# fp16 high and low parts, scaled by powers of two found on the chip, in place of 32-bit ones

## The chip, the core and the metric

The kernel runs on one core of a Trainium2 chip. The metric is the device time of one execution in microseconds (us). TensorE (PE) multiplies matrices, VectorE (DVE) and ScalarE (ACT) work elementwise, GpSimd (POOL) does small integer work and issues the gathers, SyncE (SP) issues nearly all other transfers. Every engine takes its instructions strictly in the order of the program, and waits for the others by semaphores.

## What is computed

```python
def _A_ref(x, wq, wk, wv, wo):            # attention: 32 heads of 16, one key and one value head
    q, k, v = heads(x @ wq), x @ wk, x @ wv
    p = _softmax(einsum("bhqd,bkd->bhqk", q, k) * (Dh ** -0.5), axis=-1)
    return merge(einsum("bhqk,bkd->bhqd", p, v)) @ wo

def _B_ref(x, w_q, k1, k2, u, v):         # 4096 experts, picked by two tables of 64 keys, 32 heads
    q = jnp.einsum("nd,dhc->nhc", xf, w_q)
    s1 = jnp.einsum("nhd,ed->nhe", q[..., :dk], k1)
    s2 = jnp.einsum("nhd,ed->nhe", q[..., dk:], k2)
    # the best two of s1 and of s2, and of their four sums the best two: top_s, top_e
    g = _softmax(top_s, axis=-1)
    act = _gelu(jnp.einsum("nd,nhkd->nhk", xf, u[top_e]))
    return jnp.einsum("nhk,nhk,nhkd->nd", g, act, v[top_e])

xn = _layernorm(x, axis=-1)               # x is 2048 x 512
return x + _A_ref(xn, A_wq, A_wk, A_wv, A_wo) + _B_ref(xn, B_w_q, B_k1, B_k2, B_u, B_v)
```

## The kernel before

**Stages.** The 2048 rows of x are 16 tiles of 128, in four groups of four. A prologue normalises each group, transposes it on PE (`transpose_group`) and forms keys, values and queries. Then 256 steps of attention follow (the loop over `d`, `att_steps`): in each, four pairs of score products (`scores`, L412) go to ACT, which takes their exponential (L419, 1024 columns each), and 16 products with the values (`pv`, L429) follow one step later. All other work is laid between these, by a list that the program writes out when it is built: PE gets a "fill" behind the second pair of scores of each step (`run_scores`), and ACT gets what stands in the list `ON_ACT` between the two pairs of exponentials (`mid`).

**Experts.** For the chunk `c` (four heads of eight chunks) `wp_make` multiplies the key tables into the query weights: four products (L583) of raw tiles of 512 KB (`wqt`, loaded by `wp_load` four tiles ahead into five buffers that are used in turn), four ACT copies (L584), and four transposes (L590), each of which ACT and DVE split into a high and a low part (L592, L593). These parts (`wk`) are stored to HBM (`dw`, L599) and read again for the later groups of rows (`wp_read`, L605). `item` forms the scores of one tile and one chunk in twelve products of 512 columns (L631); DVE takes the best of each head (L644, L646). For the first two groups of rows, the picked rows of u and v are gathered by index (L1091), multiplied and summed on DVE (L1103, L1138). For the other two, `dense` computes all 4096 experts: one-hot products build a table of gates (L892 to L895, L925), then for each of 32 blocks of 128 experts rows of u and v are loaded and split (`half_split`, L797, L798), multiplied with the transposed x (L833), gated, split (`high`, `low`: L1030, L1034), and multiplied with v (L971); DVE adds the results to the totals (L974).

**High and low parts.** A factor `a` of these products is held as a high part `h` and a low part `a - h`, and three of the four cross products are summed, so that twelve products stand for four. Before, the parts are 4-byte numbers (type fp32r): the rounding in the copy makes `h`, and a DVE subtraction makes the low part. Transposed x, the scores' weights, the query and key weights, u, v and the gated activations are held so.

**Transfers.** Everything that SP issues goes in order through one hardware queue (q1): among it the raw tiles, the stored and reread parts, the rows of u and v for `dense`, and for each pair of attention units a chain `dsum`, `rc`, `dinv`, `rsb` (L447 to L473) that turns the softmax's sums around through HBM for DVE's division (L478). The gathers go through a queue of their own (q0).

The names that the steps below use: `scale_factors` and `weight_squares` (prologue, one factor for the keys and queries), `wp_make` (chunks), `half_split`, `sums` and `first` (dense part), `gate`s of `batch`.

## Time and profile before

| | us |
|---|---|
| three runs, median (lowest to highest) | 1819.83 (1819.26 to 1823.11) |
| the profiled execution, its own time | 1823.24 |
| its span, first to last instruction | 1821.5 |
| of that busy: PE / DVE / ACT / POOL | 1743.2 / 1625.8 / 1290.0 / 698.9 |
| longest chain of work, share by engine | PE 48%, DVE 32%, DMA 6%, issue 4%, ACT 3% |
| moved by DMA | 478.31 MB |

The profile is that of one execution. A busy PE overlaps the modelled ends of its products, so 96% is not its peak. The trace tells the stages apart by the lines that run in them: prologue to 120 us, gathers with `wp_make` to about 320, gathers with stored parts to 560, one-hot tables to 700, the first dense part to 1010, scores of the second and fourth group to 1330, and then the one-hot and dense part of the last group.

### The profile page before, as it was taken

Reading aid. Unit: us, or ns where it says so; the run is one execution under the profiler, and the core shown is the slowest. Engines: PE = TensorE matmul, PEld = TensorE weight load, DVE = VectorE, ACT = ScalarE, POOL = GpSimd, SP = SyncE. Lnnn points to the kernel's source line nnn. Section 1 sums busy time; section 2 is a strip of 40 time slices with the busy share of each in tenths; the row PEclk is TensorE's granted clock in tenths of the full one; section 3 lists DMA queues with packets and bytes.
Section 4 is the critical chain, followed back from the end, with each engine's and each line's share of the span. In section 5 each row is a group of like instructions: output and inputs, shape, how many; then the busy total and the mean of one; then the engine's idle time right before and its main releaser. Section 6 shows DMA issues by size and latency. Waiting matters only on the chain.

```text
span 1821.5 us, 34944 instructions
## 1 busy us (share of the span) xinstructions
PE 1743.2 (96%) x10997; PEld 880.0 (48%) x10997; DVE 1625.8 (89%) x6385; ACT 1290.0 (71%) x1750; POOL 698.9 (38%) x922
## 2 busy tenths in 40 slices
PE   7999999999998889999999999999988899999998
PEld 4644444555554334555555444555543344555553
DVE  7749989999899977999999798999989778999994
ACT  5367766656568987888787565556689877888874
POOL 1124544435442122444444353345521124444440
PEclk9999999999999999999999999999999999999999
DMA  8489897996764777988899987877636768898883
GB/s 287 175 303 376 303 339 248 347 336 237 242 201 132 238 243 223 284 276 290 283 313 325 321 311 240 291 249 249 229 98 232 251 189 292 286 308 286 286 283 105
DMA packets 243705, 478.31 MB, mean 263 GB/s; under 512 B 93748, under 2 KB 117316, under 8 KB 243516
## 3 DMA queue, kind: packets, MB, share of 16 engines
q0 software_dynamic: 73728, 268.47, 43.6%
q1 hardware_dynamic: 169372, 206.93, 34.2%
q8 instruction: 87, 1.43, 0.3%
q14 instruction: 102, 0.84, 0.1%
q10 hardware_dynamic: 416, 0.66, 0.1%
HBM read 419.94 MB, written 51.15 MB: 259 GB/s over the span
## 4 chain that ended last, share of the span: by engine, by line
PE 48%; DVE 32%; DMA 6%; issue 4%; ACT 3%; POOL 1%; SPq 1%; DVEq 0%; ACTq 0%; POOLq 0%
PE psc L631 16%; PE pv L429 13%; PE sc L412 8%; DVE xa L1138 7%; DVE g L1103 6%; PE pact L833 3%; DVE oh L892 3%; PE pout L971 3%; DVE i L646 2%; DVE da L974 2%; PE pwo L527 2%; ACT pt L419 2%; DVE wk L798 1%; PE pw L583 1%; DMA rsb<-dinv 1%
## 5 line engine op out<-in xcount | busy, mean ns | idle before, releaser
L419 ACT ACTIVATE pt<-sc 128x1024 f32<-128x1024 f32 x1024 | 995.9, 1030 | 379.5 <-PE sc L412 317.8
L1091 POOL DMA_INDIRECT g<-in_uv_dram,idx x512 | 561.0, 1096 | 894.7 <-DVE xa L1138 410.7
L429 PE MATMUL pv<-pt,vaug 128*32 128x512 f32 x4096 | 494.2, 600 | 0.0
L631 PE MATMUL psc<-wk,xt 128*128 128x512 f32 x1536 | 392.8, 403 | 6.9 <-DVE i L646 1.9
L1138 DVE SCALAR_TENSOR_TENSOR xa<-g,w,xa 128x512 f32<-128x512 f32 x512 | 373.5, 748 | 0.1
L412 PE MATMUL sc<-qa,kaug 64*128 64x512 f16 x2048 | 319.6, 382 | 27.6 <-ACT pt L419 22.5
L1103 DVE CUSTOM_DVE_ANT_0 g<-g,xa 128x512 f32<-128x512 f32 x512 | 336.3, 686 | 6.0 <-DMA g<-in_uv_dram,idx 5.9
L631 PEld LDWEIGHTS psc<-wk,xt 128*128 128x128 f32 x1536 | 277.2, 188 | 112.1 <-issue 42.2
L412 PEld LDWEIGHTS <-kaug 64*128 64x128 f16 x2048 | 82.4, 94 | 346.2 <-issue 341.3
L429 PEld LDWEIGHTS pv<-pt,vaug 128*32 128x32 f32 x4096 | 107.0, 109 | 254.9 <-issue 254.9
L646 DVE FIND_INDEX8 i<-m,psc 128x8 uint32<-128x64 f32 x1024 | 207.2, 227 | 0.0
L971 PE MATMUL pout<-wk,wd 128*128 128x512 f32 x768 | 195.2, 401 | 2.7 <-DVE gy L1014 1.5
L833 PE MATMUL pact<-xt,wk 128*128 128x512 f32 x768 | 196.8, 401 | 0.6 <-DVE da L974 0.6
L971 PEld LDWEIGHTS pout<-wk,wd 128*128 128x128 f32 x768 | 140.6, 188 | 49.5 <-issue 5.6
L833 PEld LDWEIGHTS pact<-xt,wk 128*128 128x128 f32 x768 | 139.3, 188 | 49.6 <-issue 18.7
L644 DVE MAX8 m<-psc 128x8 f32<-128x64 f32 x1024 | 146.5, 218 | 10.5 <-PE psc L631 10.1
L798 DVE TENSOR_TENSOR wk<-rw,wk 128x512 fp32r<-128x512 f32 x128 | 85.6, 688 | 8.1 <-ACT wk L797 8.1
L974 DVE TENSOR_TENSOR da<-da,pout 128x512 f32<-128x512 f32 x128 | 82.8, 685 | 6.2 <-PE pout L971 6.2
L892 DVE TENSOR_TENSOR oh<-oh 128x2048 f16<-128x2048 f16 x64 | 78.1, 1220 | 3.3 <-issue 1.9
L646 DVE MATCH_VALUE_LOAD i<-m,psc 128x8 f32 x1024 | 77.7, 76 | 0.0
L797 ACT CAST wk<-rw 128x512 fp32r<-128x512 f32 x128 | 74.4, 636 | 0.0
L690 POOL CAST fi<-i 128x64 f32<-128x64 uint32 x32 | 9.0, 281 | 136.7 <-DVE i L646 131.8
(179 smaller groups left out, 1341.9 us busy)
## 6 DMA issues: line engine op xcount, KB each, us to landing
wk<-dw SPq DMA_DIRECT2D x96, 512.0 KB
wqt<-in_wqT_dram SPq DMA_DIRECT2D x32, 512.0 KB
dw<-wk SPq DMA_DIRECT2D x32, 512.0 KB
rw<-in_ub_dram SPq DMA_DIRECT2D x64, 256.0 KB
rw<-in_vb_dram SPq DMA_DIRECT2D x64, 256.0 KB
gy<-dg SPq DMA_DIRECT2D x64, 256.0 KB
dg<-gst SPq DMA_DIRECT2D x14, 928.0 KB
g<-in_uv_dram,idx POOLq DMA_INDIRECT x512
```

What stands on the lines that cost most here:

```text
L412: nc.tensor.matmul(p[:, b, :], kaug[o:o + 64, kc * P:(kc + 1) * P], QA[u][o:o + 64, i, :], start=True, stop=True)
L419: nc.scalar.activation(PT[u, kc, i], p, AF.Exp, scale=SCALE)
L429: nc.tensor.matmul(PV[u][32 * j:32 * j + 32, :], vaug[:, kc, :], pt[:, b, :], start=kc == 0, stop=kc == 15)
L631: nc.tensor.matmul(p, XT[k][:, a, j * P:(j + 1) * P], WC[n_][k][:, bb, :], start=n == 0, stop=n == 11)
L644: nc.vector.max(m8[:, jb, s, :], p[:, s * E:(s + 1) * E])
L646: nc.vector.max_index(i8[:, jb, s, :], m8[:, jb, s, :], p[:, s * E:(s + 1) * E])
L833: nc.tensor.matmul(p, us[:, a, k * P:(k + 1) * P], XT[k][:, c, :], start=n == 0, stop=n == 11)
L892: nc.vector.tensor_tensor(out=oa, in0=num(P), in1=bc(0, tb, P), op=OP.is_equal)
L971: nc.tensor.matmul(p, wd[0][:, a, j * P:(j + 1) * P], vs[:, c, :], start=n == 0, stop=n == 5)
L1091: nc.gpsimd.indirect_dma_start(out=gt, out_offset=None, in_=uv, in_offset=bass.IndirectOffsetOnAxis(ap=IDX[ph, c, ti][:, s:s + 1], axis=0))
L1103: nc.vector.tensor_tensor_reduce(u, u, XN[TPH * ph + ti], scale=1.0, scalar=0.0, op0=OP.mult, op1=OP.add, accum_out=a[:, i:i + 1])
L1138: nc.vector.scalar_tensor_tensor(acc, v, w[:, i:i + 1], acc, op0=OP.mult, op1=OP.add)
```

## The change

All these parts become 2-byte fp16. Since fp16 holds a narrow range of sizes, each factor is first multiplied by a power of two that the kernel finds from norms of the data. Rows of x are scaled by 1024 in the normalisation. For the query and key weights, sums of squares give the factors (`scale_factors`, now ahead of the first split, with the products inside the first `transpose_group`). For each chunk of the raw tiles ACT sums squares (`wp_square`, 32 times, 1024 columns) and a small product on PE and three DVE operations make the factor (`wp_factors`). For u and v, all 4096 rows of `uv` (16 MB) are read once in 16 transfers of 1 MB in steps 8 to 38 of the attention, ACT sums their squares (64 times, 512 columns), and `norm_factors` makes the factors at step 43. Copies that made high parts become activations with a scale from a column of `cols`; subtractions that made low parts, and the additions of L974, become `scalar_tensor_tensor` with such a column. The inverse factors enter where values leave the products: in the exponential's, the square's and tanh's scale and in constants. The stored parts `dw` and `dxt` take half the bytes. Products with fp16 are issued as two instructions, LDWEIGHTS and MATMUL.

```diff
+XUP = 1024.0
+GDOWN = 2.0 ** -20
-    d_xt = [[dram.tile([P, 2, 512], F32, name=f"dxt{g}_{k}") for k in range(KC)] for g in range(1, NGRP)]
+    d_xt = [[dram.tile([P, 2, 512], F16, name=f"dxt{g}_{k}") for k in range(KC)] for g in range(1, NGRP)]
-    d_w = [dram.tile([P, KC, 2, 512], F32, name=f"dw{c}") for c in range(NC)]
+    d_w = [dram.tile([P, KC, 2, 512], F16, name=f"dw{c}") for c in range(NC)]
...
-                xt = big.tile([P, 2, 512], F32R, name="xt", bufs=4)
+                xt = big.tile([P, 2, 512], F16, name="xt", bufs=4)
...
     def scale_factors():
+        for k in range(KC):
+            nc.tensor.matmul(q, ones, sk[:, k, :], start=k == 0, stop=k == KC - 1)
+        nc.tensor.matmul(r, ones, st, start=True, stop=True)
         for k in range(KC):
             nc.tensor.matmul(p, ones, sq[:, k, :], start=k == 0, stop=k == KC - 1)
...
+        factors(x[:, :3], col(S_WQ, 3), col(I_Q, 3), ())
...
+    def wp_square():
+        n = squared[0]
+        squared[0] += 1
+        nc.scalar.activation(junk, WC["raw", n // 4, n % 4], AF.Square, accum_out=squares[:, n % 4:n % 4 + 1])
+
+    def wp_step(c, n=None):
+        if factored[0] < squared[0] // 4:
+            wp_factors()
+        if n is not None:
+            while squared[0] <= n:
+                wp_square()
+        n = squared[0]
+        if n < 4 * (c + 2) and n // 4 == factored[0] and ("raw", n // 4, n % 4) in WC:
+            wp_square()
+
+    def wp_factors():
+        c = factored[0]
+        factored[0] += 1
+        p = xtile("pn")[:, :1]
+        for h in range(4):
+            nc.tensor.matmul(p, ones_f, squares[:, h:h + 1], start=h == 0, stop=h == 3)
+        x = small.tile([P, 1], F32, name="xw")
+        nc.scalar.activation(x, p, AF.Copy, scale=col(K2))
+        factors(x.bitcast(I32), col(S_W + c), col(I_W + c), ())
...
     def wp_make(c):
...
                 if ("raw", n // 4, n % 4) not in WC:
                     wp_load(n // 4, n % 4)
+            wp_step(c, 4 * c + h)
             w = WC.pop(("raw", c, h))
...
-            nc.scalar.copy(wk[:, 0, :], p)
-            low = lambda p=p, wk=wk: nc.vector.tensor_tensor(out=wk[:, 1, :], in0=p, in1=wk[:, 0, :], op=OP.subtract)
+            nc.scalar.activation(wk[:, 0, :], p, AF.Copy, scale=col(S_W + c))
+            low = lambda p=p, wk=wk: nc.vector.scalar_tensor_tensor(wk[:, 1, :], p, col(S_W + c), wk[:, 0, :],
+                                                                    op0=OP.mult, op1=OP.subtract)
...
         def half_split(b, i):
             rw, w = raws[b], wk_tile()
-            nc.scalar.copy(w[:, 0, :], rw[:, i, :])
-            behind(lambda: nc.vector.tensor_tensor(out=w[:, 1, :], in0=rw[:, i, :], in1=w[:, 0, :], op=OP.subtract))
+            f = col(S_U + i)
+            nc.scalar.activation(w[:, 0, :], rw[:, i, :], AF.Copy, scale=f)
+            behind(lambda: nc.vector.scalar_tensor_tensor(w[:, 1, :], rw[:, i, :], f, w[:, 0, :],
+                                                          op0=OP.mult, op1=OP.subtract))
...
-                nc.vector.tensor_add(acc, acc, p)
+                stt(acc, p, col(C_OUT), acc, op0=OP.mult, op1=OP.add)
...
+    def norm_rows(j):
+        t = late[0].tile([P, 2, 2 * D], F32, name="un", tag="wd", bufs=2)
+        nc.sync.dma_start(t, uv[2 * j * P:2 * (j + 1) * P, :].rearrange("(r p) d -> p r d", p=P))
+        return t
+
+    def norm_sums(j, t):
+        for r in range(2):
+            for i in range(2):
+                v = t[:, r, i * D:(i + 1) * D]
+                nc.scalar.activation(v, v, AF.Square, accum_out=norms[:, i, 2 * j + r:2 * j + r + 1])
...
+    def norm_steps(d):
+        if d >= 8 and d % 2 == 0 and d // 2 - 4 < NB // 2:
+            NU[d // 2 - 4] = norm_rows(d // 2 - 4)
+        j = d // 2 - 5
+        if d % 2 == 1 and j in NU:
+            t = NU.pop(j)
+            on_act(lambda: norm_sums(j, t))
+        if d == 2 * (NB // 2 + 5) + 1:
+            norm_factors()
```

Two places of the order of instructions that the prediction speaks of. The first is ACT about 40 us into the attention, in the fourth chunk of `wp_make`: `pt` are the exponentials, `wt` the copies of the chunk's products. Before:

```order
L419 ACTIVATE pt_2049<-sc_2046 128x1024
L419 ACTIVATE pt_2054<-sc_2051 128x1024
L584 COPY wt_2065<-pw_2069 128x512
L419 ACTIVATE pt_2098<-sc_2095 128x1024
L419 ACTIVATE pt_2103<-sc_2100 128x1024
L1119 ACTIVATE gth_2113<-gy_2033 128x4
L683 ACTIVATE ex_1986<-mx_1983 128x16
L419 ACTIVATE pt_2142<-sc_2139 128x1024
L419 ACTIVATE pt_2147<-sc_2144 128x1024
L584 COPY wt_2065<-pw_2151 128x512
L584 COPY wt_2066<-pw_2164 128x512
```

Now, the same stretch, with `junk,squares` the sums of squares of raw tiles:

```order
L450 ACTIVATE pt_2124<-sc_2121 128x1024
L608 ACTIVATE junk_162,squares_163<-wqt_2137 128x1024
L645 COPY wt_2135<-pw_2140 128x512
L450 ACTIVATE pt_2169<-sc_2166 128x1024
L450 ACTIVATE pt_2174<-sc_2171 128x1024
L1184 ACTIVATE gth_2184<-gy_2103 128x4
L746 ACTIVATE ex_2056<-mx_2053,cols_159 128x16
L450 ACTIVATE pt_2213<-sc_2210 128x1024
L450 ACTIVATE pt_2218<-sc_2215 128x1024
L608 ACTIVATE junk_162,squares_163<-wqt_2220 128x1024
L645 COPY wt_2135<-pw_2223 128x512
L608 ACTIVATE junk_162,squares_163<-wqt_2234 128x1024
```

Each copy now has a square of a raw tile ahead of it, and that tile is the one four places on in the loads, which is the tile whose transfer the program issues in the same place.

The second place is SP at the same time: `wqt` are the raw tiles, `dw` the stored parts, `un` the rows of u and v that are read for their norms. Before:

```order
L599 DMA dw2_90<-wk_2007 128x1024
L567 DMA wqt_2067<-in_wqT_dram 128x2x512
L567 DMA wqt_2149<-in_wqT_dram 128x2x512
L567 DMA wqt_2162<-in_wqT_dram 128x2x512
L567 DMA wqt_2236<-in_wqT_dram 128x2x512
L447 DMA dsum_102<-e_2189 4x512
```

Now:

```order
L662 DMA dw2_90<-wk_2077 128x1024
L598 DMA wqt_2137<-in_wqT_dram 128x2x512
L598 DMA wqt_2220<-in_wqT_dram 128x2x512
L598 DMA wqt_2234<-in_wqT_dram 128x2x512
L1298 DMA un_2244<-in_uv_dram 128x2x1024
L598 DMA wqt_2311<-in_wqT_dram 128x2x512
```

The raw tiles stand where they stood, behind the last part stored, and a transfer of 1 MB has come between the third and the fourth of them; such a transfer now stands in every second step.

More of the change, by code (lines that the diff above doesn't have):

```diff
@@ L197, in transpose_group @@
             XK.setdefault(g, []).append(xt)
+            between(k)
             if not first:
@@ L203, in tile_kernel, with factors @@
     FIRST = ((0, 0), (1, 0), (0, 1))
-    sqk = const.tile([P, 2], F32, name="sqk")
+    cols = const.tile([P, 40], F32, name="cols")
+    col = lambda i, n=1: cols[:, i:i + n]
+    S_WQ, S_WKV, X_2, I_Q, I_KV, X_5, K2, G_QK, C_Q, C_K, S_Q, S_K = range(12)
+    S_U, S_V, C_SQ, C_TANH, C_OUT = range(12, 17)
+    S_W, I_W = 24, 32
+    def factors(x, scale, inverse, more):
+        nc.vector.tensor_scalar(x, x, 24, 23, op0=OP.logical_shift_right, op1=OP.logical_shift_left)
+        nc.vector.tensor_scalar(scale.bitcast(I32), x, -1.0, 205.0 * ONE, op0=OP.mult, op1=OP.add)
+        for out, power in ((inverse, -10),) + more:
+            nc.vector.tensor_scalar(out.bitcast(I32), x, (49.0 + power) * ONE, None, op0=OP.add)
     qmax = const.tile([P, NGRP], F32, name="qmax")
@@ L293, in weight_squares @@
             nc.scalar.activation(sq[:, 2 * i:2 * i + 2, :], wraws[i], AF.Square)
[L294 to L300 removed]
+            if i == 0:
+                sk = PK["ksq"] = start.tile([P, KC, 32], BF16, name="wksq")
+                nc.scalar.activation(sk, wkv_f, AF.Square)
+                st = PK["tsq"] = start.tile([P, 2 * E], BF16, name="ktsq")
+                nc.scalar.activation(st, kTs.rearrange("p s e -> p (s e)"), AF.Square)
@@ new lines, in scale_factors, with balance @@
+        x = most.bitcast(I32)
+        factors(x[:, :3], col(S_WQ, 3), col(I_Q, 3), ())
+        PK["exponents"] = x
+    def balance():
+        x = PK.pop("exponents")
+        d = start.tile([P, 1], I32, name="xd")
+        nc.vector.tensor_tensor(out=d, in0=x[:, 2:3], in1=x[:, 0:1], op=OP.subtract)
+        nc.vector.tensor_scalar(d, d, 0.5, 127.0 * ONE, op0=OP.mult, op1=OP.add)
+        sq, sk = col(S_Q).bitcast(I32), col(S_K).bitcast(I32)
+        nc.vector.tensor_single_scalar(sq, d, EXPONENT, op=OP.bitwise_and)
+        nc.vector.tensor_scalar(sk, sq, -1.0, 254.0 * ONE, op0=OP.mult, op1=OP.add)
+        nc.vector.tensor_mul(cols[:, C_Q:C_Q + 2], cols[:, S_Q:S_Q + 2], cols[:, I_Q:I_Q + 2])
+        nc.vector.tensor_mul(col(G_QK), col(I_Q), col(I_KV))
@@ L1027, in high @@
                 if not both:
-                    both.append(late[0].tile([P, 4, 512], F32R, name="wd", tag="wd", bufs=2))
+                    both.append(late[0].tile([P, 4, 512], F16, name="wd", tag="wd", bufs=2))
                 wd.append(both[0][:, 2 * half:2 * half + 2, :])
```

128 lines of the change are left out of this document (70 added, 58 removed).

## The prediction

> **What bounds the kernel now.** I read first the page's head, then the busy time of each engine in slices of 50 us, then the chain of work that ended last, stage by stage.
>
> ```profile
> span 1821.5 us, 34944 instructions
> PE 1743.2 (96%) x10997; PEld 880.0 (48%) x10997; DVE 1625.8 (89%) x6385; ACT 1290.0 (71%) x1750; POOL 698.9 (38%) x922
> ```
>
> PE is busy for nearly all of the span, which alone says little. The slices (busy us of 50 with instruction counts, then the granted clock, the DMA engines' share and GB/s) show three kinds of stage:
>
> ```profile
> 150.00:200.00 50.00, 49.04 (x289) 21.21 (x289) 46.41 (x238) 34.78 (x48) 25.25 (x36) 1.00 0.96 352
> 400.00:450.00 50.00, 50.00 (x301) 26.22 (x294) 46.48 (x308) 30.10 (x38) 23.31 (x50) 1.00 0.74 255
> 1600.00:1650.00 50.00, 49.81 (x288) 27.07 (x289) 50.00 (x121) 41.42 (x61) 22.47 (x20) 1.00 0.90 288
> ```
>
> At 150 and 400 us PE is full and DVE has 3.5 us of 50 left. At 150 us the transfers are full too (0.96), ACT has 15 us left. At 1600 us, in the second dense part, DVE is full and PE only seems so. The clock is 1.00 in all three. The chain says the same; of each stage, the shares of its own length:
>
> ```profile
> by line: PE psc L631 31.9%; PE pv L429 23.0%; PE sc L412 13.0%; PE pw L583 10.6%; DVE xa L1138 3.7%; issue 3.3%; PE pwt L590 2.9%; DVE i L646 2.9%; DVE g L1103 2.7%; DVE m L644 1.9%; DVE wk L593 1.7%; ACT pt L419 0.9%; ACT wk L592 0.8%; DVE
> by line: PE psc L631 37.2%; PE pv L429 17.7%; PE sc L412 10.6%; DVE i L646 8.0%; DMA rsb<-dinv 5.8%; DVE m L644 5.2%; DVE xa L1138 3.9%; DVE g L1103 3.5%; issue 1.6%; POOL e L730 0.7%; ACT pt L419 0.5%; POOL fi L690 0.4%; POOL ii L731 0.4%;
> by line: DVE xa L1138 12.2%; PE pact L833 10.7%; PE pout L971 9.5%; PE pv L429 9.3%; DVE g L1103 9.2%; issue 5.7%; PE sc L412 5.7%; DMA dinv<-rc 5.5%; DVE da L974 4.5%; ACT pt L419 3.4%; DMA rsb<-dinv 3.2%; DVE gy L1017 3.2%; DVE wk L798 3.
> by line: PE psc L631 43.9%; PE pv L429 23.7%; PE sc L412 14.0%; PE pwo L527 4.5%; DMA rsb<-dinv 3.1%; DVE i L646 3.0%; DVE xa L1138 2.5%; DVE g L1103 2.3%; DVE m L644 2.0%; DVE on L478 0.2%; PE pact L833 0.2%; DVE gy L1113 0.1%; DVE gg L711
> by line: DVE xa L1138 14.8%; DVE g L1103 12.9%; issue 8.8%; PE pact L833 7.7%; PE pv L429 7.4%; PE pout L971 6.5%; DVE da L974 5.3%; DMA g<-in_uv_dram,idx 5.3%; PE sc L412 4.5%; DVE wk L798 4.5%; DVE gy L1017 3.4%; DVE gy L1014 3.2%; POOL g
> ```
>
> In order: gathers with `wp_make`; gathers with stored parts; first dense part; second scoring stage; second dense part. In the first, second and fourth PE sets the pace, and ACT is on the chain for 2% at most; in the fifth DVE does; in the third both.
>
> **The change part by part.** Sums are against the profiled execution (1823.24 us, span 1821.5); it lies 0.2% above the median of 1819.83, and the sum is carried over to the median.
>
> *Faster products.* How much sooner one product follows another:
>
> ```profile
> L631 PE MATMUL psc<-wk,xt 128*128 128x512 f32 x1536 | 392.8, 403 | 6.9 <-DVE i L646 1.9 <-DMA wk<-dw 1.3 <-DVE m L644 1.1
> L833 PE MATMUL pact<-xt,wk 128*128 128x512 f32 x768 | 196.8, 401 | 0.6 <-DVE da L974 0.6
> L971 PE MATMUL pout<-wk,wd 128*128 128x512 f32 x768 | 195.2, 401 | 2.7 <-DVE gy L1014 1.5 <-DVE wd L1034 0.8 <-DVE da L974 0.3
> L302 PE MATMUL pws<-wsq,ones 128*128 128x512 bf16 x4 | 1.0, 382 | 0.0
> L925 PE MATMUL pg<-oh 128*128 128x64 f16 x960 | 37.9, 193 | 12.0 <-DVE oh L895 11.9
> 402.03 4.41 PE L631 MATMUL psc<-wk,xt 128*128 128x512 f32 x18
> 17.05 1.04 PE L302 MATMUL pws<-wsq,ones 128*128 128x512 bf16 x4
> ```
>
> Eighteen fp32r products took 4.41 us, the last of them 0.403, so one starts every (4.41 - 0.403) / 17 = 0.236 us. The four bf16 products of the prologue, also 128 by 512, each with its own weight load: (1.04 - 0.382) / 3 = 0.219. The trace has no fp16 product of full size; this is the nearest row. The gain is between 0 and 0.017 us a product, and I take 0.014. That fp16 needs two instructions costs nothing: the 960 fp16 pairs of L925 came every 37.9 / 960 = 0.039 us. Some 3300 products change (1536 + 768 + 768 and those of the prologue), 46 us in all, but only what lies on the chain counts. With 0.24 us each, the chain holds 82 us of L631 in 340 to 560 (37.2% of 220), about 340 products, 4.8 us; 140 us in 1010 to 1330, 585 products, 8.2 us; 63 us of L833 and L971 in 700 to 1010, 260 products, 3.7 us; 70 us in 120 to 340, 4.1 us. DVE is close behind in all of these (3.5 us of 50), so I take half in the second stage (-2.4), two thirds in the fourth, where DVE has more room (-5.4), half in the first dense part (-1.8), and nothing but 0.5 in the last.
>
> *DVE operations with a column as factor.* 128 of L798, 128 of L974 and 32 of L593 turn from a plain add or subtract to an operation with a scalar read from a column, which L1138 already is:
>
> ```profile
> L1138 DVE SCALAR_TENSOR_TENSOR xa<-g,w,xa 128x512 f32<-128x512 f32 x512 | 373.5, 748 | 0.1
> L974 DVE TENSOR_TENSOR da<-da,pout 128x512 f32<-128x512 f32 x128 | 82.8, 685 | 6.2 <-PE pout L971 6.2
> L798 DVE TENSOR_TENSOR wk<-rw,wk 128x512 fp32r<-128x512 f32 x128 | 85.6, 688 | 8.1 <-ACT wk L797 8.1
> 411.23 2.07 DVE L1138 SCALAR_TENSOR_TENSOR xa<-g,w,xa 128x512 f32<-128x512 f32 x3
> 1613.35 1.88 DVE L974 TENSOR_TENSOR da<-da,pout 128x512 f32<-128x512 f32 x3
> ```
>
> One of L1138 starts every (2.07 - 0.748) / 2 = 0.661 us, one of L974 every (1.88 - 0.685) / 2 = 0.598. So each costs 0.063 more, and each dense part, with 64 and 64 of them, 8.1 us of DVE. In the second nearly all of it is on the chain: +7. In the first, where DVE has half of the chain: +4. ACT's copies become scaled ones too, but ACT is not bound there.
>
> *Half the bytes.* Loads and stores of split parts shrink to half. Two waits of DVE for a small transfer stood behind such loads in SP's queue:
>
> ```profile
> 486.45 0.67 SPq L473 DMA_DIRECT2D rsb<-dinv  x1
> 499.21 0.69 DVE L478 TENSOR_TENSOR on<-ot,rsb 128x512 f32<-128x512 f32 x1 [4.48 <-DMA rsb<-dinv]
> 1008.95 0.67 SPq L473 DMA_DIRECT2D rsb<-dinv  x1
> 1019.07 0.69 DVE L478 TENSOR_TENSOR on<-ot,rsb 128x512 f32<-128x512 f32 x1 [9.92 <-DMA rsb<-dinv]
> ```
>
> `rsb` was 12.8 us on its way at 486 us and 10.1 at 1009, and DVE stood idle for 4.48 and 9.92 us. With half the bytes ahead of it most of that goes; next late are DVE's own queue and PE. Between 0 and 14.4; I take two thirds: -3 in the second stage, -6.6 in the fourth.
>
> *Prologue.* The factor now precedes the split: two squares, reductions and five small operations stand ahead of the high parts.
>
> ```profile
> 9.36 1.14 ACT L1347 CAST wqs<-g 128x512 fp32r<-128x512 f32 x2 [1.12 <-DMA g<-in_wq_dram]
> 14.77 2.01 ACT L293 ACTIVATE wsq<-g 128x1024 bf16<-128x1024 f32 x2
> 18.12 0.69 DVE L306 TENSOR_REDUCE most<-pws 128x1 f32<-128x512 f32 x1 [1.32 <-PE pws L302]
> ```
>
> Before, ACT split the weights at 9.36 us, as soon as they had come. Now 2.0 us of squares, 0.7 of the long reduction and about 1 of small ones come first, while PE transposes anyway; the first products come some 2.5 us later. The 60 products of each of four groups give 3.4 back, and the new small ones cost 1: zero.
>
> *Squares of the raw tiles and of u and v: the step that decides.* 22 of the 32 squares of 1024 columns (1.05 us each by L293) and the norms' groups of four (4 x 0.57 by the casts, 2.3 us) fall into the attention, on an engine whose exponentials PE awaits at once. ACT's gaps, and the loads:
>
> ```profile
> 155.18 1.94 ACT L419 ACTIVATE pt<-sc 128x1024 f32<-128x1024 f32 x2 [0.92 <-PE sc L412]
> 157.39 0.59 ACT L584 COPY wt<-pw 128x512 f32<-128x512 f32 x1 [0.26 <-PE pw L583]
> 159.35 1.94 ACT L419 ACTIVATE pt<-sc 128x1024 f32<-128x1024 f32 x2 [1.37 <-PE sc L412]
> 161.86 1.95 ACT L419 ACTIVATE pt<-sc 128x1024 f32<-128x1024 f32 x2 [0.38 <-PE sc L412]
> 163.69 0.59 ACT L584 COPY wt<-pw 128x512 f32<-128x512 f32 x1
> 165.51 0.59 ACT L584 COPY wt<-pw 128x512 f32<-128x512 f32 x1 [1.23 <-PE pw L583]
> 166.82 1.94 ACT L419 ACTIVATE pt<-sc 128x1024 f32<-128x1024 f32 x2 [0.72 <-PE psc L631]
> 157.09 8.78 SPq L567 DMA_DIRECT2D wqt<-in_wqT_dram  x4
> q1 hardware_dynamic: 3406, 8.05, 41.6%
> ```
>
> From 157.12, the end of one pair of exponentials, to 159.35 ACT had 1.64 us besides the copy; from 163.81 to 166.82 it had 1.95 besides two. Now a square stands ahead of each copy, so one or two in such a gap. Work alone, from 120 to 290 us: 22 squares and 8 groups of norms, 41 us, against about 16 gaps of 1.8 us and 8 of 0.4, 32: 9 us over. Behind a late square stand the next exponentials. PE waits 0.4 us later than they do (the bracket at 161.86): its next score products need the two PSUM buffers that the exponentials empty, and in all 14 such places that takes 5 off.
>
> The rest is a wait for data. Each square reads a raw tile that SP's queue is asked for in the same place of the program: before, nobody read it for another chunk, some 30 us. The queue moved 8.05 MB in 50 us, so 512 KB take 3.3 us alone, and the 256 KB of `rsb` above took up to 12.8 behind others. I take 5: its own time and half of one transfer ahead. Of the 16 such squares (chunks five to eight), three open a chunk, where the load is only issued with the copies (157.09 against 157.12), and wait 4; five stand second in a gap, on a tile whose buffer is only freed by the product just before, and wait 5 less a square, a copy and the queue's lead, 2.6; the other eight have most of a step (7 us) and wait 0.5, since the 1 MB of u and v is now ahead of some. That is 12 + 13 + 4 = 29 us. With 9 - 5 and 4.1 us less of PE, 29; not every delay is passed on whole, and I take nine tenths: **+26**. Without any wait it would be 0, with a lag of 8 us 60 instead of 29, so +54.
>
> *Factors of u and v.* At step 43 PE's small product waits for a DVE reduction that stands behind the search of a whole tile, its maxima and then their indices, which take longer:
>
> ```profile
> 403.74 1.15 DVE L644 MAX8 m<-psc 128x8 f32<-128x64 f32 x8 [1.42 <-PE psc L631]
> ```
>
> That is +3, once.
>
> Sum: 0 + 26 + (-2.4 - 3 + 3) + (4 - 1.8) + (-5.4 - 6.6) + (7 - 0.5) = **+20 us**, 1843 for the profiled execution, 1840 against the median.
>
> **The rivals.**
>
> *The gaps swallow it (faster).* If the raw tiles are there when ACT comes, the stage from 120 us costs nothing. Then the other terms are left, and with the products' gain passed on whole in the scoring stages (-4.8 and -8.2) and both DVE waits gone, the sum is 0 - 6.3 + 2.2 - 18.1 + 6.5 = -16: 1804. For it: ACT has 15 of 50 us free. Against it: order and issue times put load and square side by side. It decides below about 6 us of delay in that stage, which is what the other terms give back in the forecast. 0.27.
>
> *Longer waits.* The transfers there run at 0.96 already; 16 MB more come in while the stores give back less than half. With 8 us of lag the sum is +48: 1868. 0.16.
>
> *No faster products.* If fp16 streams at fp32r's pace, the 4.1 + 2.4 + 1.8 + 5.4 + 0.5 = 14 us are gone: 1854. For it: only four bf16 products, early in the program, speak for a gain. Against it: their 0.219 beside 0.236. 0.12. The Trainium skill (page FP8 and Floating Point Precision, section TensorE Precision Notes) has fp16 "upconverted to FP22" and 4-byte numbers of reduced precision cut to the same FP22, so that both would go through the array alike. By that rule the time is this rival's; the trace, with 0.219 beside 0.236, does not agree, as far as bf16 stands for fp16.
>
> *They cancel.* Between the first rival and the forecast there is a stretch within 0.2%: 0.07.
>
> **How the numbers follow.** The forecast has 0.38: 1840. What can be told from no change is about 0.2%, 3.6 us. Faster: the first rival, less its near edge, 0.25. Same: 0.09. Slower: the rest, 0.66. The ends of the unknown costs, all low (no delay at 120 us, whole gains, half of DVE's price hidden in each dense part) and all high (a lag of 8 us, no faster products, no wait of DVE saved), give some 1797 and 1893; a tenth of the chance is left out at each side, on the low side by the first rival's own far half: 1799 to 1870. The forecast by itself, with a lag of 4 to 6 us (waits of 19 to 39) and 3 us more for the other terms, is 1828 to 1852.
>
> **What would show it.** Right: L631 and L833 every 0.22 us; the raw tiles' squares with idle time before them put down to their transfer, some 30 us together; the stretch of the first two units of attention longer by 25 us; both waits of `rsb` smaller; L974 and L798 near 0.745 us. Wrong: squares without idle time before them (first rival); waits for `g` on DVE (the gathers late, the transfers full); L631 still at 0.236. The forecast falls if ACT reaches the squares later than I think, since PE's delay then lets the tiles land.

## The result, and the profile after

The changed kernel takes 1877.24 us (median of 4 runs, 1870.76 to 1878.94), the kernel before 1819.55 beside it: a ratio of 1.031 (1.028 to 1.034). It is 58 us slower, where 20 were forecast, and lies outside the range. The profiled execution took 1878.94 us. Its page's head, with the clock of the 40 slices:

```profile
span 1877.2 us, 35271 instructions
PE 1721.3 (92%) x11064; PEld 606.3 (32%) x11064; DVE 1646.4 (88%) x6424; ACT 1387.9 (74%) x1951; POOL 709.2 (38%) x923
PEclk9999988999999999999999999999999999999999
```

PE has less to do (1721 us, 1743 before), and the clock shows two slices, 235 to 328 us, below 0.9. Slices of 50 us (columns as in the prediction) show the place:

```profile
100.00:150.00 50.00, 45.11 (x230) 15.53 (x226) 23.70 (x85) 34.18 (x51) 13.16 (x14) 0.93 0.81 282
150.00:200.00 50.00, 42.27 (x253) 14.72 (x252) 37.46 (x191) 34.79 (x55) 17.93 (x23) 0.93 0.78 278
200.00:250.00 50.00, 40.41 (x231) 14.54 (x230) 35.91 (x192) 35.85 (x61) 16.30 (x22) 0.90 0.72 257
250.00:300.00 50.00, 38.72 (x217) 12.76 (x216) 32.76 (x164) 36.37 (x68) 18.67 (x23) 0.90 0.74 260
300.00:350.00 50.00, 40.67 (x212) 12.55 (x212) 33.82 (x169) 33.95 (x60) 14.19 (x20) 0.83 0.65 227
```

PE, full at 150 us before (49.04), stands idle for 5 to 11 us of each 50. ACT is no busier at 150 us than before (34.79, 34.78), the transfers are less busy (0.65 to 0.81 against 0.96), and the clock fell. So an order of waits is late, not an engine full. The waits of ACT and of PE over the whole run (total, times, longest) name it:

```profile
ACT junk L608 <- DMA wqt<-in_wqT_dram: 33.9, 11, 6.3
PE sc L443 <- ACT pt L450: 49.0, 70, 5.4
PE pn L625 <- ACT junk L608: 4.4, 4, 1.7
```

The kernel before had no such squares, and of PE's waits for the exponentials less than half:

```profile
PE sc L412 <- ACT pt L419: 22.5, 43, 2.0
```

Of the 49.0 us, 24.1 lie between 120 and 340 us, where the kernel before has no such wait.

One such stall of the changed kernel in order of time (start, duration; in brackets the idle time before and what ended it):

```profile
229.19 1.08 PE L644 MATMUL pw<-wqt,kTs 128*64 128x512 f32 x4
230.74 1.92 PE L460 MATMUL pv<-pt,vaug 128*32 128x512 f32 x16
234.67 1.06 ACT L608 ACTIVATE junk<-wqt 128x1024 bf16<-128x1024 f32 x1 [5.30 <-DMA wqt<-in_wqT_dram]
235.73 0.57 ACT L645 COPY wt<-pw 128x512 f32<-128x512 f32 x1
236.19 1.94 ACT L450 ACTIVATE pt<-sc 128x1024 f32<-128x1024 f32 x2
237.27 0.61 PE L443 MATMUL sc<-qa,kaug 64*128 64x512 f16 x2 [4.61 <-ACT pt L450]
238.73 2.74 PE L694 MATMUL psc<-wk,xt 128*128 128x512 f16 x6
```

ACT stands 5.30 us before a square whose tile is on its way; the copy and the exponentials queue behind it, and PE, out of score buffers, waits 4.61. Then six products take 2.74 us, where six take 1.47 at full clock (a row further down): after such a stall PE runs at half.

The exponentials are the same in all kernels, four to a step, so the start of the first one in step d gives the delay of that step against the one profile of the kernel before. Differences over the stretches, in us:

| | predicted | measured |
|---|---|---|
| up to step 0 (prologue) | 0 | +8.0 |
| steps 0 to 28 (squares, norms) | +26 | +56.7 |
| steps 28 to 64; of that steps 40 to 44 (factors of u, v) | -2.4; +3 | -3.4; +5.8 |
| steps 64 to 72 (one-hot tables begin) | 0 | +3.5 |
| steps 72 to 136 (first dense part) | +2.2 | +1.6 |
| steps 136 to 184 (scoring) | -12 | -13.0 |
| step 184 to the end (second dense part) | +6.5 | +2.2 |
| sum | +20.3 | +55.7 |

Two stretches at the start make the whole error. The groups of lines that the prediction's other steps named (busy time, mean ns):

```profile
L694 PE MATMUL psc<-wk,xt 128*128 128x512 f16 x1536 | 363.2, 385 | 10.4 <-DVE wk L655 6.4 <-ACT wt L645 3.8 <-DVE i L709 0.3
L862 DVE SCALAR_TENSOR_TENSOR wk<-rw,cols,wk 128x512 f16<-128x512 f32 x128 | 92.7, 741 | 5.8 <-ACT wk L861 5.8
L1040 DVE SCALAR_TENSOR_TENSOR da<-pout,cols,da 128x512 f32<-128x512 f32 x128 | 90.3, 740 | 5.5 <-PE pout L1037 5.5
L608 ACT ACTIVATE junk<-wqt 128x1024 bf16<-128x1024 f32 x32 | 33.9, 1060 | 33.9 <-DMA wqt<-in_wqT_dram 33.9
L1305 ACT ACTIVATE un<-un 128x512 f32<-128x512 f32 x64 | 39.4, 628 | 0.0
465.36 4.06 PE L694 MATMUL psc<-wk,xt 128*128 128x512 f16 x18
```

Eighteen fp16 products take 4.06 us: one every (4.06 - 0.385) / 17 = 0.216, where fp32r took 0.236. DVE's operations with a column take 0.740.

### The profile page after: what moved, and what is told of

Its sections match the earlier page's. It is cut to its first block, busy times and chain, and to the rows that moved or that the text cites. A ratio compares the mean times of both kernels' runs of the same rounds, so it can differ in the third digit from the quotient of the medians.

```text
span 1877.2 us, 35271 instructions
## 1 busy us (share of the span) xinstructions
PE 1721.3 (92%) x11064; PEld 606.3 (32%) x11064; DVE 1646.4 (88%) x6424; ACT 1387.9 (74%) x1951; POOL 709.2 (38%) x923
## 4 chain that ended last, share of the span: by engine, by line
DVE 52%; PE 25%; DMA 7%; issue 4%; ACT 4%; POOL 1%; SPq 1%; DVEq 0%; ACTq 0%; POOLq 0%
DVE xa L1203 11%; DVE g L1168 10%; PE pv L460 7%; DVE i L709 6%; PE psc L694 6%; DVE m L707 4%; PE sc L443 4%; DVE oh L957 3%; DMA wqt<-in_wqT_dram 3%; DVE da L1040 3%; ACT pt L450 2%; DVE wk L862 2%; PE pwo L558 2%; PE pact L898 2%; PE pout L1037 2%
## 5 line engine op out<-in xcount | busy, mean ns | idle before, releaser
L694 PE MATMUL psc<-wk,xt 128*128 128x512 f16 x1536 | 363.2, 385 | 10.4 <-DVE wk L655 6.4
L694 PEld LDWEIGHTS <-xt 128*128 128x128 f16 x1536 | 142.0, 99 | 215.1 <-issue 68.3
L1037 PE MATMUL pout<-wk,wd 128*128 128x512 f16 x768 | 180.3, 382 | 19.5 <-DVE gy L1079 9.0
L898 PE MATMUL pact<-xt,wk 128*128 128x512 f16 x768 | 183.4, 385 | 9.5 <-DVE da L1040 9.1
L1037 PEld LDWEIGHTS <-wd 128*128 128x128 f16 x768 | 72.9, 98 | 116.5 <-issue 29.9
L898 PEld LDWEIGHTS <-wk 128*128 128x128 f16 x768 | 71.5, 99 | 109.0 <-issue 34.9
L862 DVE SCALAR_TENSOR_TENSOR wk<-rw,cols,wk 128x512 f16<-128x512 f32 x128 | 92.7, 741 | 5.8 <-ACT wk L861 5.8
L1040 DVE SCALAR_TENSOR_TENSOR da<-pout,cols,da 128x512 f32<-128x512 f32 x128 | 90.3, 740 | 5.5 <-PE pout L1037 5.5
L861 ACT ACTIVATE wk<-rw,cols 128x512 f16<-128x512 f32 x128 | 86.7, 731 | 0.0
L1191 DVE SCALAR_TENSOR_TENSOR w<-gth,ga 128x4 f32<-128x4 f32 x128 | 19.9, 155 | 58.0 <-ACT gth L1184 58.0
```

The costliest lines, as they stand in the source:

```text
L694: nc.tensor.matmul(p, XT[k][:, a, j * P:(j + 1) * P], WC[n_][k][:, bb, :], start=n == 0, stop=n == 11)
L898: nc.tensor.matmul(p, us[:, a, k * P:(k + 1) * P], XT[k][:, c, :], start=n == 0, stop=n == 11)
L1037: nc.tensor.matmul(p, wd[0][:, a, j * P:(j + 1) * P], vs[:, c, :], start=n == 0, stop=n == 5)
L1040: stt(acc, p, col(C_OUT), acc, op0=OP.mult, op1=OP.add)
```

## The experiments

Each kernel below is the changed kernel but for the edit shown. Times are medians, ratios are those to the kernel before on the same chip. The kernels ran on several chips, and each ratio's interval reaches 2 to 6 us to either side, so a difference of two medians is good to some 5 us. Where steps are spoken of, delays are counted as in the table above, from one profiled execution each.

**Order or amount?** Four kernels: later squares, no norms, no squares, and nothing that finds a factor.

```diff
-        if n < 4 * (c + 2) and n // 4 == factored[0] and ("raw", n // 4, n % 4) in WC:
-            wp_square()
+            if late[0] is None or n <= 4 * c + at + 1:
+                wp_square()
```

Here `at` is the step's place in its chunk, 0 to 7.

> The same work on every engine; in the attention a raw tile is squared three places of the order after its load was asked for (before: at the same place). Theory 'waiting' (ACT stands behind raw tiles that are still on their way, 33.9 us in the changed kernel, then PE idles and its clock is halved): that wait falls under 8 us, the clock in 100 to 350 us is near 1.00 again, and the time is about 1835 (40 of the 56 us that steps 0 to 26 lost). Theory 'volume' (ACT has too much to do in that stretch, whenever it does it): 1868 to 1880, the wait for the tile merely changes its name. Theory 'queue' (16 MB more on SP's queue make everything late): 1860 to 1877.

Measured: 1851.11 us, 1.0148 (1.0129 to 1.0167), 26 less than the changed kernel (29 by the ratios). No square waits for a transfer any more. Of PE's waits for the exponentials this is left, first over the whole run; then, between 120 and 340 us alone, these and the waits of the small products for a square:

```profile
PE sc L443 <- ACT pt L450: 32.7, 67, 2.0
```

```profile
PE pn L626 <- ACT junk L608: 4.3, 3, 2.3
PE sc L443 <- ACT pt L450: 3.5, 7, 1.0
```

Steps 0 to 28 lose 22.4 us instead of 56.7. So the wait behind the transfers is 34 us of that stretch, and what is left has no wait for a transfer in it: between the theories, both have their part.

```diff
+    nc.gpsimd.memset(norms, 1.45)
...
-            NU[d // 2 - 4] = norm_rows(d // 2 - 4)
+            pass
```

> Leaves out the reads of u and v for their norms and the 64 squares over them (the norms are a constant; the factors are still formed from it at step 43). 'Waiting': ACT is relieved of 37 us, of which gaps held about half, and the raw tiles still come late: 1858 to 1866. 'Volume': 1835 to 1845. 'Queue': with 16 MB less ahead of them the raw tiles are there, the wait for wqt falls from 33.9 to under 15 us: 1835 to 1845.

Measured: 1874.86 us, 1.0297 (1.0276 to 1.0317), only 2.4 less. The wait has not changed:

```profile
ACT junk L608 <- DMA wqt<-in_wqT_dram: 33.9, 8, 8.7
```

With 16 MB less ahead of them the tiles come no sooner: those that ACT waited for were there 3.6 to 8.6 us after they were asked for in the changed kernel (median 6.5), and 3.6 to 8.9 here (median 5.2). The theory of a full queue falls. Also, 39 us of ACT's squares (L1305) left and the median hardly moved, less than each theory said. The profiled execution says more: it was the fastest of four (1869.26; the others 1874.02 to 1880.45), and its steps 0 to 28 lost 42.4 us, 14 less than in the changed kernel.

```diff
+    nc.gpsimd.memset(squares, 2.56)
...
-        nc.scalar.activation(junk, WC["raw", n // 4, n % 4], AF.Square, accum_out=squares[:, n % 4:n % 4 + 1])
```

> Leaves out the 32 squares of the raw tiles (their sums are a constant; the products and small operations that make the factors from it stay). 'Waiting': 1825 to 1835, since the wait for wqt and the halved clock go with them, and some 3 us in the prologue. 'Volume': 34 us of ACT less, of which two thirds count: 1850 to 1858. 'Queue': 1855 to 1870.

Measured: 1835.07 us, 1.0072 (1.0055 to 1.0089), 42 less. The profiled execution was the fastest of five (1822.48; the others 1834.89 to 1837.46), with the clock at 1.00 from 100 to 350 us; in it steps 0 to 28 lost 4.4 us and the prologue 1.1. Over the run its granted clock was 0.994, that of the four others 0.986 to 0.988, so these two figures are this kernel's best case.

```diff
+        nc.gpsimd.memset(cols[:, a:b], v)
...
-            wp_step(c, 4 * c + h)
...
-            wp_step(c)
...
-            norm_steps(d)
```

The first line, at the start, sets S_W, I_W, S_U, S_V, C_SQ, C_TANH and C_OUT.

> All factors of the scoring weights and of u and v are constants: no squares, no norms, no reads of u and v, no small products for them; the prologue's factors for wq and wkv stay. If the finding of the factors is the whole loss, the other terms of the prediction are left: +8 of the prologue at most 4, steps 44 to 64 -8, scoring -12 to -15, column operands of DVE +6 to +9: 1800 to 1812. If the fp16 form itself costs something in steps 0 to 26, as its slower DVE operations or another clock, 1820 to 1835.

Measured: 1808.48 us, 0.9926 (0.9909 to 0.9942), 69 less, and 0.7% faster than before. The fp16 form costs nothing in steps 0 to 28: they gain 4.9 us. All of the loss is the finding of factors. By the medians the parts don't add: no norms is worth 2, no squares 42, both and the small products 69. That the norms' squares sit partly in ACT's waiting for tiles would explain it, but isn't shown: in the profiled executions steps 0 to 28 gain 14 us without the norms, 52 without the squares and 62 without both.

**The halved clock.** Zeros added into attention's open sums keep PE at work where it stood idle longest.

```diff
+    def keep_busy(u, n):
+        for _ in range(n):
+            nc.tensor.matmul(PV[u][:32, :], zeros, XT[0][:, 0, :], start=False, stop=False)
...
+            if d in (7, 13, 17, 21):
+                keep_busy(pu, BUSY[d])
```

> The changed kernel, with 101 more products on TensorE (zeros into attention's open sums, 0.22 us each) at the six places where it stood idle for 2.8 to 5.4 us between 170 and 320 us (in steps 7, 11, 13, 17, 19 and 21), 10 to 22 of them at each. Nothing is taken away from ACT or from the transfers. Theory 'clock' (a good part of the loss is TensorE at half clock after such an idle stretch): the granted clock between 100 and 360 us stays whole there, half-clock time falls from 51 us to under 25, and the time falls by 8 to 18 us, to 1859 to 1869. Rival 'waits alone' (what TensorE gains it waits for again, since the transfers land when they land): the clock is whole, the time stays at 1872 to 1880, and the wait for wqt grows by what the clock gave.

Measured: 1873.3 us, 1.029 (1.0265 to 1.0315); 106 products stood in the trace, since step 11 had two such places and step 19 none. The stall shown above, in this kernel, then its windows, then its waits of ACT:

```profile
231.09 4.26 PE L470 MATMUL pv<-xt,zeros 128*32 128x512 f16 x19
235.29 0.60 PE L443 MATMUL sc<-qa,kaug 64*128 64x512 f16 x4
235.83 1.47 PE L705 MATMUL psc<-wk,xt 128*128 128x512 f16 x6
```

```profile
200.00:250.00 50.00, 49.08 (x299) 18.20 (x298) 36.56 (x197) 37.00 (x66) 15.80 (x21) 1.00 0.68 239
```

```profile
ACT junk L617 <- DMA wqt<-in_wqT_dram: 30.1, 11, 6.6
```

Half-clock time between 100 and 360 us, by the records of the granted clock, fell from 51.2 to 17.1 us. The time fell by 4, within the spread of both: the interval takes in the changed kernel's own 1.031. DVE did no more in those 50 us than in the changed kernel (36.56, 35.91). By its time the rival holds (1872 to 1880), though the wait for tiles did not grow as it said. The stretch itself speaks for 'clock': steps 0 to 28 lost 47.4 us instead of 56.7, while the second dense part, where no zeros stand, lost 6 us more than in the changed kernel (8.3, 2.2). So what these 34 us at half clock cost by themselves lies between nothing, by the intervals' ends, and some 9 us: the smaller part of the loss in any case.

**Columns in the dense parts.**

```diff
-            f = col(S_U + i)
+            f = 2048.0
...
-                stt(acc, p, col(C_OUT), acc, op0=OP.mult, op1=OP.add)
+                stt(acc, p, 2.0 ** -12, acc, op0=OP.mult, op1=OP.add)
```

> The factors of u and v are still found, but the dense parts' split of the rows and their sums take constants in place of the columns (128 + 128 operations of VectorE back at the shape with an immediate factor). The prediction priced the columns at 4 + 7 us: then the time falls to about 1866. By the times at which steps 64 and 248 were reached, the columns cost VectorE what it has to spare: 1872 to 1879.

Measured: 1867.52 us, 1.0255 (1.0223 to 1.0287), 10 less. So the columns cost about the 11 us that were predicted, as far as six executions from 1859.18 to 1878.31 tell, though the steps' delays in the dense parts showed only 1.6 and 2.2 (here -1.4 and -2.4): something else gains in the same stretches.

**The norms elsewhere, and squares that wait for nothing.**

```diff
     def norm_steps(d):
+        d -= 14
...
-        if d == 2 * (NB // 2 + 5) + 1:
-            norm_factors()
+        k = d - 2 * (NB // 2 + 5) - 1
+        if 0 <= k < 3:
+            norm_factors(k)
```

`norm_factors` now does the maximum, the product and the factors in a step each.

> Squares of the raw tiles three places after their load, as in the run with late squares; besides, the reads and squares for the norms of u and v begin 14 steps later (steps 22 to 57), and the small product for their factors is issued a step after VectorE's maximum and its use a step after that. 'Waiting' with the stretch of steps 0 to 28 as the only crowded one: norms cost nothing where they now lie, steps 0 to 28 lose 8 to 14 us instead of 22, the factors 0 to 1 instead of 5: 1832 to 1840. If the norms cost the same 10 us wherever they lie: 1845 to 1852.

Measured: 1830.67 us, 1.0048 (1.0031 to 1.0065), 20 less than late squares alone (18 by the ratios). Steps 0 to 28 lose 8.2, steps 28 to 64 gain 8.1 although 56 of the 64 squares for the norms now lie there, and the factors cost nothing (-1.5 in steps 56 to 60, where they now lie). So 28 squares, moved out of the crowded stretch (36 lay there, 8 still do), were worth 14 us there, and 14 steps later they cost at most 2 (steps 28 to 64 gain 9.8 without any).

```diff
-        nc.scalar.activation(x, p, AF.Copy, scale=col(K2))
+        nc.scalar.activation(x, p, AF.Copy, scale=2.0)
...
             nc.scalar.copy(wt[h // 2][:, h % 2, :], p)
+            nc.scalar.activation(junk, p, AF.Square, accum_out=squares[:, h:h + 1])
```

Here `wp_square` and `wp_step` are gone, and the norms are as in the run before.

> A factor of the scoring weights is found from the squares of the products themselves (each 128x512 tile is squared from PSUM right behind its copy, 32 operations of about 0.6 us, in place of 32 of 1.06 us on raw tiles); norms of u and v as in the run with late norms. No square waits for a transfer any more: steps 0 to 28 lose 2 to 6 us, the prologue under 5, and the time is 1812 to 1824. If ACT's volume in steps 0 to 28 were what counts: 22 us there instead of 37 + 20, some 1835.

Measured: 1821.93 us, 1.0005 (0.9991 to 1.0018): as fast as the kernel before, with all factors still found on the chip. The prologue lost nothing (-0.3), steps 0 to 28 8.0, two more than forecast. Between 100 and 330 us two waits of ACT stood out:

```profile
ACT wk L637 <- DVE cols L220: 4.4, 6, 1.2
ACT xw L609 <- PE pn L607: 3.6, 5, 1.1
```

**The way from the last square to the factor.**

```diff
-        for h in range(4):
-            nc.tensor.matmul(p, ones_f, squares[:, h:h + 1], start=h == 0, stop=h == 3)
+        nc.tensor.matmul(p, ones_f, squares, start=True, stop=True)
...
+        nc.vector.reduce_sum(x, p, axis=AX.X)
```

It is issued two pieces of `item` after the chunk's last product.

> As the run with norms of the products, but the small product for a chunk's factor is issued one step earlier than its use (one product of four columns in place of four of one, and VectorE instead of ScalarE takes its sum). Theory 'chain': in the run before, ACT stood 3.6 us before xw and 4.4 us before the first scaled copy of a chunk, with the exponentials queued behind it; both waits go and with them 6 to 9 us: 1813 to 1816, faster than the kernel before. Rival: those 8 us lie where ACT would have waited for TensorE anyway, as with the halved clock: 1819 to 1823, the waits before the exponentials grow by as much.

Measured: 1821.89 us, 1.0006 (0.9992 to 1.002): nothing. In the same window:

```profile
ACT wk L646 <- PE pwt L644: 11.3, 7, 4.3
ACT wk L646 <- DVE cols L220: 4.1, 2, 2.4
```

The wait for xw is gone, the one for `cols` is not (4.1 us), and ACT's wait for the transposes grew to 11.3 us (7.8 in the run before). The time is the rival's: taking away ACT's wait for xw gave PE nothing. As one of the two waits stayed, the theory of the chain isn't settled by this run.

```diff
+        nc.gpsimd.memset(cols[:, a:b], v)
...
-        p = xtile("pn")[:, :1]
-        for h in range(4):
-            nc.tensor.matmul(p, ones_f, squares[:, h:h + 1], start=h == 0, stop=h == 3)
-        x = small.tile([P, 1], F32, name="xw")
-        nc.scalar.activation(x, p, AF.Copy, scale=col(K2))
-        factors(x.bitcast(I32), col(S_W + c), col(I_W + c), ())
```

> The changed kernel without the small products and operations that make a chunk's factor (it is a constant); the squares of the raw tiles, the norms and their place stay. 'Chain': the prediction left this path out (TensorE's product waits for the last square, ACT for the product, VectorE's four operations and ACT again), and it costs 1 to 1.5 us a chunk with the exponentials behind it: 1862 to 1868, the prologue 3 us less. Rival: the next raw tile is waited for all the longer: 1872 to 1877.

Measured: 1871.16 us, 1.0285 (1.0264 to 1.0306), 6 less than the changed kernel (4 by the ratios). The time lies between the two theories, the stretches speak for 'chain': the prologue ended 5.7 us earlier, twice what was said, and steps 0 to 28 lost 48.2, 8.5 less, which is 1.4 us for each of the six chunks there. The wait for the tiles did not grow as the rival said (32.4 us, 33.9 in the changed kernel).

**The pieces together.** The run with the early factor, but u and v with the constant 2 to the 11th, once as an immediate operand (the diff) and once in columns set at the start.

```diff
-            f = col(S_U + i)
+            f = 2048.0
...
-            norm_steps(d)
```

> As the run with the early factor, but u and v take one constant factor, 2 to the 11th, as an immediate operand: no reads and squares for norms, no columns in VectorE's 256 operations (it holds while the entries of u and v stay below 32). If the terms found so far add up (run with the early factor 1821 to 1822, columns -9 to -12, norms and their factors -2 to -4): 1806 to 1811, faster than the kernel before. If columns and norms lie in time that is waited out anyway: 1817 to 1822.

> The same, with the constants held in columns, so that VectorE's 256 operations read their factor from memory as in the changed kernel: against the run with immediates this is the price of the columns alone. By the 0.055 us of one operation, 256 of them, and the prediction's share that is hidden: 9 to 12 us slower than the run with immediates, 1816 to 1822. Rival: TensorE is the later engine there now and again, 2 to 6 us.

Measured: 1802.77 us, 0.9903 (0.9882 to 0.9924), with immediates, below the 1806 to 1811 of the summed terms; 1819.53 us, 0.9988 (0.9976 to 1.0001), with columns. The groups of the first, then of the second:

```profile
L855 DVE SCALAR_TENSOR_TENSOR wk<-rw,wk 128x512 f16<-128x512 f32 x128 | 86.8, 702 | 6.1 <-ACT wk L854 6.0
L1033 DVE SCALAR_TENSOR_TENSOR da<-pout,da 128x512 f32<-128x512 f32 x128 | 84.3, 706 | 5.1 <-PE pout L1030 5.1
```

```profile
L857 DVE SCALAR_TENSOR_TENSOR wk<-rw,cols,wk 128x512 f16<-128x512 f32 x128 | 95.0, 770 | 5.9 <-ACT wk L856 5.9
L1035 DVE SCALAR_TENSOR_TENSOR da<-pout,cols,da 128x512 f32<-128x512 f32 x128 | 92.3, 768 | 4.3 <-PE pout L1032 4.3
```

A column costs 0.065 us an operation, 256 of them 16.6, and the kernels differ by 16.8 (each interval leaves some 4 us): as far as this tells, nothing of it is hidden, more than either theory said. (DVE's durations differ between chips: the same operation took 740 ns on one, 746 on another and 770 on this one.) The norms, which both drop, are then worth 2 to 3 us (1821.89 and 1.0006 with them, 1819.53 and 0.9988 without), though the intervals overlap. The kernel with immediates is 1% faster than the one before. It holds only while entries of u and v stay below 32 in size.

## Why the prediction went wrong, point by point

*Squares: "Without any wait it would be 0".* This failed, and it is the larger half of the error. The wait itself was sized well: 29 us forecast, 33.9 measured (in sum: eleven squares waited 0.6 to 6.3 us each, where sixteen were to wait 0.5 to 4), and taking it away gave 34 in the stretch (26 in the median). But steps 0 to 28 lose 22 us without any wait for a transfer. The work was counted as "9 us over" less the "5" that the score buffers absorb, and PE's gain was set against it. The runs show what was left out of that count: with the norms moved, the late squares lose 8.2 where the kernel without any finding gains 4.9. So norms in that stretch were 14 us and squares with their small products 13, not 4 together. Five of the 13 are the small products themselves (5.0 us of PE in steps 0 to 28), for which the step has no term. Summing free ACT time over the stretch was the mistake: what stands behind a square waits for it, whatever free time comes later. It is not the exponentials above all that wait: with late squares PE is idle for 25 us in steps 0 to 28 (10 before), and only 3.5 of these end with an exponential. 4.3 are waits of the small products for a square, 4.4 waits for the copies `wt` and the factor's `xw`, and 3.8 (0.7 before) waits for low parts, as DVE itself waits longer for the high parts from ACT (18.2 us, 5.3 before).

The halved clock has a part in it. PE's instructions between the first exponentials of steps 4 and 28 (us, each profile's sum of matmul time and the gaps between):

| | length | PE busy | PE idle | at half clock |
|---|---|---|---|---|
| before | 173.8 | 167.3 | 6.5 | 0 |
| changed | 226.6 | 185.0 | 41.6 | 46.4 |
| zeros added | 219.1 | 196.3 | 22.8 | 13.7 |
| late squares | 191.0 | 173.1 | 17.9 | 13.7 |
| late squares, late norms | 180.1 | 168.0 | 12.1 | 3.4 |
| no finding | 169.9 | 161.8 | 8.1 | 3.4 |

The length grew by 53: PE is idle for 35 more and busy for 18 more (the small products are some 5 of these), although its fp16 products are shorter, since for 46 us it ran at half clock. The prediction knew only of the idle time. With the half clock down to 14 us (third line, where 22.7 of the busy time are the zeros) PE's own products take 11 us less than in the changed kernel, and the stretch is 7 shorter: idle time and zeros together grew by 4.

*Prologue: "zero".* The step counted the squares ahead of the first split and gave the new small products 1 us. It has no term for the eight raw tiles that ACT squares there, nor for PE's wait at the products `pn` that need these squares. Two of the five rows of the changed kernel there:

```profile
38.99 0.38 PE L625 MATMUL pn<-squares,ones_f 128*128 128x1 f32 x2 [1.14 <-ACT junk L608]
...
49.56 0.38 PE L625 MATMUL pn<-squares,ones_f 128*128 128x1 f32 x2 [1.03 <-ACT junk L608]
```

The five wait 4.6 us together, and two windows of half clock follow. Without the squares the prologue is late by 1.1, without the products by 2.3, with squares over the products by -0.3. It was the place again: four steps of `wp_make` stand in a row there, and ACT's squares pile up ahead of the product.

*Factors of u and v, +3.* Right in kind, +5.8 in size: PE waited for the maximum that stood behind DVE's search.

```profile
479.74 0.59 PE L1311 MATMUL pn<-um,ones_f 128*128 128x2 f32 x2 [4.05 <-DVE um L1309]
```

*Faster products.* Right: 0.216 us instead of 0.236. Steps 28 to 64 gain 9.8 us without the finding (-5.4 forecast), so this and the end of DVE's wait for `rsb` arrive about whole: 4.8 and 4.5 us were their full sizes, of which the prediction took half and two thirds. No run tells the two apart. The rival without faster products falls. The Trainium skill (page FP8 and Floating Point Precision, section TensorE Precision Notes) brings both types to FP22, from which the prediction read one pace for both; the trace does not agree with that reading, with 0.216 beside 0.236.

*Columns.* The direction was right, the price too low: 11 us forecast, 10 by the run with constants in the changed kernel and 17 by the last pair. The gains of the other side were too low as well: with immediates steps 72 to 136 gain 7.0 and the stretch from step 184 on 2.5, where "-1.8" and "0.5" stood. So the sum +2.2 came near the measured +1.6, and +6.5 not too far from +2.2, by two errors that offset, which is luck. Whether these gains are PE's or the halved transfers' was not tried.

*Scoring stage.* -12 forecast, -13.0 measured. DVE's waits for `rsb` behind `dinv`, 14.4 us before, are gone from the list of waits. The match is no better than some 4 us, though: in the first four runs, all on one chip, the stretch gains 7.7 to 9.6 against the same profile of the kernel before, and 11.2 to 13.2 in all the others.

*A wait nobody named.* At step 64 PE now comes to the one-hot tables ahead of POOL:

```profile
622.97 1.09 PE L923 MATMUL ptd<-ident,da 128*128 128x128 f32 x8 [3.22 <-POOL da L801]
```

In the kernel before:

```profile
559.72 0.55 PE L858 MATMUL ptd<-ident,da 128*128 128x128 f32 x3 [1.13 <-POOL da L738]
```

That stretch loses 3.5 us in the changed kernel and 2.4 to 5.2 in all the others: where POOL is late, PE waits for what it gained before, as it seems; no run takes this wait away.

*What stays open.* Steps 0 to 28 still lose some 8 us in the runs with squares over the products, with only 2.6 us of PE's waits put down to the exponentials. Without any norms the two last runs still lose 4.7 and 5.8 there, so the first norms, at steps 22 to 28, may be 2 to 3 of the 8. Beside the kernel without any finding PE is busy 9.3 us longer there, 5.7 of it in the small products; with the early factor these fell to 1.1, but PE's idle time grew by 4.3, and the stretch stayed as long. What sets its pace then was not found. Nor is the halved clock's own price known better than from nothing to some 9 us: executions of one kernel with a lower granted clock took longer (without squares 0.994 and 1822.48, 0.986 to 0.988 and 1834.89 to 1837.46), but that doesn't tell which makes the other.

## What to carry to other kernels

Work given to an engine with free time costs what stands behind it at that place, so look at the next instructions in its queue, and who waits for them, and not at the sum of its gaps: 28 squares cost 14 us in one place and at most 2 some 14 steps later. A load should be read several steps after it is asked for, and a norm is cheapest over data that is in hand anyway. When two disturbances share a stretch, the total can hide what one of them costs (2 us in the median for the norms, 14 in their stretch); take both away, then each alone, and read the stretch. On an engine that is full, the form of an operand counts: a factor from a column instead of an immediate one cost 0.065 us 256 times, and all of it.

## What the hardware showed besides

The granted clock falls without PE being idle for long. In the changed kernel's records it changes on a grid of 3.41 us. Of the windows at full clock, all 17 in which PE was busy for at most 46% (1.6 us) were followed by half clock, and the lowest that was not had 50%; only two others, of 65 and 68%, were followed by it. It came back after windows with 88% or more, and stayed at half after the seven of 36 to 82%. The Trainium skill (page TensorE: Matmul & The Clock Gate, section "Why this matters for your kernels") asks for no idle gaps over about 3 us; here single gaps of 1.3 to 1.8 us, each beside a shorter one in the same window, were enough.

ACT's sum along a row is an instruction of its own: each square with a sum is followed by one of 0.20 us.

```profile
L1305 ACT ACTIVATION_READ_ACCUMULATOR un<-un 128x1 f32 x64 | 12.8, 200 | 0.0
```

The next instruction starts 0.09 us after its start, so 96 of them took about 9 us of ACT.
